# VectorE in source order in units 1 to 7 of a block-scheme MLP on one Trainium2 core

## The chip, the core and the metric

The kernel runs on one core of a Trainium2 chip. The metric is the device time of one execution in microseconds (us). TensorE (PE; its weight loads are listed apart, as PEld), VectorE (DVE), ScalarE (ACT), GpSimd (POOL) and SyncE (SP, here only the issuer of DMAs) run at the same time and wait for each other through semaphores. Each engine starts its own instructions in the order in which they stand in its queue.

## What is computed

Windowed attention, then an MLP over tokens and channels, then a normalised MLP over channels. The change touches only the last one:

```python
mu = np.mean(x, axis=-1, keepdims=True)
var = np.mean((x - mu) ** 2, axis=-1, keepdims=True)
xn = (x - mu) / np.sqrt(var + 1e-06) * g_ln
ch = np.maximum(xn @ w_ch1, 0.0) @ w_ch2      # 512 -> 2048 -> 512
return x + ch
```

with x of 2 x 768 rows and 512 channels, all in float32. On TensorE each float32 operand stands as a high and a low part, so one product takes three matmuls (`mm3`, L300 to L304).

## The kernel before

The normalised MLP is the second half of the program. Its 2048 hidden channels are cut into 8 pieces (`NP`), its rows into two halves; a **unit** is one piece for one half, so there are 16. Units 0 to 7 (`unit`, L770) take the first half, units 8 to 15 (`unit1`, L857) the second.

A unit of the first half forms its hidden block by a scheme of seven products of 2x2 blocks. Step k (0 to 6) issues product k (six matmuls of 384 columns into one PSUM bank, `product`, L755), then the readers of that bank, then `flow` (L818): two of the twelve `second` blocks (three matmuls of 512 columns each, for the second matrix of the unit before; one block only in steps 5 and 6), and then `step(k)` (L1265). The bank readers are: step 0 a copy on ACT (L787), all others adds of 384 columns on DVE (L775): `um` in step 1, `sm` in step 2, `wm` in step 3, `sm` in step 4, `wm` and `um` in step 5, `um` in step 6. After steps 2, 4, 5 and 6 a finished block goes through `relu` (L762): ACT writes the high part `ah` (L766), DVE the low part `al` (L767), which the next unit's `second` blocks read.

The products rotate over two PSUM banks (`ps_mm`), so product k+2 waits for the readers of product k. The transposes `tx` of `prep_x` (L595) take a bank of the same pool: in a step with a `tx` the next product comes back to the bank of the product just done.

`step(k)` holds the side work. `convert_all(2)` takes two pieces of the decoding and splitting of weights, which lasts until unit 2 (DVE: L150, L152, L156, L158, L237, L242, L247, the sums L265 to L271 and L282; ACT: L133 to L139, L209 to L213, L277; these last need spill buffers that a DMA to DRAM frees). `start` and `finish` take one piece of `bg`: in unit 1 the statistics `norm_stats` of groups 2 and 3 (L528; three BN_STATS with their aggregate, and then a chain of seven small operations of three columns, with a square root on ACT in it) and the first normalisation; in units 2 to 5, in steps 1 and 5, one piece of `prep_x` (L583): transposes on PE, then on ACT the copy `f` (L599), three normalisations of the next piece (L562) and one cast for each operand (L580), and on DVE the subtraction that gives its low part (L581) and the sums `t` (L610 to L622). From unit 2, step 6, `next(sums)` takes pieces of `w2_sums` (L715): seven pieces for each of the 8 parts, on DVE the sums `wx` (L726, from a weight tile that a DMA brought), `wt` (L735 to L738) and the low part `wk` (L748), whose DMA to DRAM stands behind it.

Who sets the order: PE and ACT stand under `manual_schedule` in this part (L1200, L1258), which puts them in the order of the source. DVE does not: there a scheduler orders the instructions at build time by priority and by its own estimate of when each is ready, and `high_priority(URGENT)` (L784) lifts the bank readers and `relu`. SP's order of DMAs is the scheduler's too.

Of the kernel before, what the change touches and what calls it, by code (L numbers as in the profile page):

```python
# [17 lines left out]
ALU = mybir.AluOpType  # L18
# [28 lines left out]
NP = F2 // 2  # L47
RING = 12
URGENT = 400
MS = ("B11", "T2", "B21", "T1", "B22", "T3", "T4")  # L50
EARLY = 16
NEG = -8e9
# [4 lines left out]
def f32(ap):  # L57
    return ap.bitcast(F32)


class Kern:
# [693 lines left out]
    def product(self, n, s, k, ps):  # L755
        w = self.ring_w1(n)
        x = self.operand(s, MS[k])
        for e in range(2):
# [3 lines left out]
    def relu(self, key, x):  # L762
        nc = self.nc
        ah = self.ap.tile([P, GN], F32R, tag="ah", name=f"ah_{key}")
        al = self.ap.tile([P, GN], F32R, tag="al", name=f"al_{key}")
        nc.scalar.activation(ah, x, AF.Relu)  # L766
        nc.vector.scalar_tensor_tensor(al, x, 0.0, f32(ah), op0=ALU.max, op1=ALU.subtract)  # L767
        return ah, al

    def unit(self, n, pending, step):  # L770
# [7 lines left out]
        for k in range(7):  # L778
# [4 lines left out]
            urgent = ExitStack()  # L783
            urgent.enter_context(self.tc.high_priority(URGENT))  # L784
            if k == 0:
# [57 lines left out]
    def pieces(self, name, x, relu=False):  # L843
        ah = self.ap.tile([P, GN], F32R, tag="ah", name=f"ah_{name}")
        al = self.ap.tile([P, GN], F32R, tag="al", name=f"al_{name}")
        self.cut(ah, al, x, relu)
        return ah, al

    def cut(self, hi, lo, x, relu):
        nc = self.nc  # L850
        nc.scalar.activation(hi, x, AF.Relu if relu else AF.Copy)
        if relu:
            nc.vector.scalar_tensor_tensor(lo, x, 0.0, f32(hi), op0=ALU.max, op1=ALU.subtract)
        else:
            nc.vector.tensor_tensor(lo, x, f32(hi), op=ALU.subtract)

    def unit1(self, n, pending, step):  # L857
# [8 lines left out]
        for k in range(7):  # L866
# [4 lines left out]
            urgent = ExitStack()  # L871
            urgent.enter_context(self.tc.high_priority(URGENT))
            if k == 0:
# [222 lines left out]
    def run(self):  # L1096
        tc, nc, ctx = self.tc, self.nc, self.ctx
# [73 lines left out]
        E = mybir.EngineType  # L1171
# [25 lines left out]
        later, pending = deque(), deque()  # L1197
# [63 lines left out]
        sums = (x for p in (2, 3, 4, 5, 0, 6, 1, 7) for x in self.w2_sums(p))  # L1261
        pending.popleft()()
        for n in range(2 * NP):

            def step(k):  # L1265
                if n == 0 and k == 6:
                    for r in range(9, RING):
                        self.load_w1(r)
                self.convert_all(2)
                if (n, k) == (4, 0):  # L1270
                    self.read_again(0)
                if n == 1 or n in range(2, 6) and k in (1, 5):
                    for _ in range(2 if n == 1 and k > 4 else 1):
                        self.start(1)
                        self.finish()

                if n > 2 or n == 2 and k > 5:
                    for _ in range((2, 0, 1, 2, 2, 0, 2)[k] if n < 6 else 2 if n == 7 or k in (0, 4) else 1):
                        next(sums, None)

            if n == 1:
                self.bg += [self.norm_stats(2)] * (GT + 1) + [self.norm_stats(3)] * (GT + 1)
                self.bg += [self.prep_x(1)] * 9
            pending = (self.unit1 if n >= NP else self.unit)(n, pending, step)
        self.tail(pending)


# [84 lines left out]
```

## Time and profile before

| | us |
|---|---|
| median of 3 runs (lowest, highest) | 580.86 (580.39, 584.26) |
| the profiled execution | 581.19 |
| its span, first to last instruction | 579.4 |
| PE busy in the span | 562.0 (97%) |
| DVE busy | 425.4 (73%) |
| ACT busy | 297.2 (51%) |

The page lists busy times by engine, then groups of instructions by line. The timeline gives single instructions with start, duration and, in brackets, the idle time of the engine before them and what ended it. Units 1 to 7 lie between 330.25 and 447.3 us of the span.

### The profile page before, as it was taken

The page shows a single profiled execution, that of the slowest core. Times are in us where ns is not written, and L with a number is a line of the kernel's source. Part 1 is how long each engine was busy: PE and PEld are TensorE (multiplying, and loading weights), DVE is VectorE, ACT ScalarE, POOL GpSimd, SP SyncE. Part 2 cuts the span into 40 slices and gives each one's busy share as a digit, 9 for nine tenths or more (in the row PEclk, how much of TensorE's full clock was granted, in tenths as well). Part 3 has the DMA queues.
Part 4 walks back from the last instruction along what each step waited for, and adds up shares of the span by engine and source line. Part 5 has one row for each costly group of instructions (what it writes and reads, how often), then busy time and mean ns, then how long its engine had stood idle before and what let it go on. Part 6 is the DMA issues. An engine that isn't in the chain of part 4 may idle for free.

```text
span 579.4 us, 10272 instructions
## 1 busy us (share of the span) xinstructions
PE 562.0 (97%) x3656; PEld 494.7 (85%) x3656; DVE 425.4 (73%) x1012; ACT 297.2 (51%) x629; POOL 22.2 (4%) x54
## 2 busy tenths in 40 slices
PE   8798998999999999999999999999999999999997
PEld 3465776889998889998988888888899999999997
DVE  5598966576887689756659898786986786677781
ACT  5598757326875654755578464463432232233320
POOL 0314400000000000000000000000000000000000
PEclk9799999999999999999999999999999999999999
DMA  8999910133668766788936899897988998777545
GB/s 278 330 315 286 282 66 2 33 113 110 229 206 271 255 219 232 274 314 290 326 111 234 278 325 334 268 334 233 306 261 280 329 292 297 237 226 232 186 155 172
DMA packets 61993, 137.88 MB, mean 238 GB/s; under 512 B 5875, under 2 KB 19955, under 8 KB 61942
## 3 DMA queue, kind: packets, MB, share of 16 engines
q1 hardware_dynamic: 61936, 137.21, 71.4%
q8 instruction: 29, 0.48, 0.3%
q14 instruction: 22, 0.18, 0.1%
q10 hardware_dynamic: 6, 0.02, 0.0%
HBM read 102.60 MB, written 34.60 MB: 237 GB/s over the span
## 4 chain that ended last, share of the span: by engine, by line
PE 80%; DVE 8%; DMA 6%; ACT 4%; issue 1%; POOL 0%; SPq 0%; DVEq 0%; ACTq 0%; POOLq 0%
PE m L302 6%; PE m L304 6%; PE m L303 6%; PE g L475 3%; PE acc_x L303 2%; PE acc_x L304 2%; PE acc_x L302 2%; DMA slot<-w2s 2%; PE acc_y L304 2%; PE acc_y L303 2%; PE acc_y L302 2%; PE av L446 2%; ACT pr L419 1%; DMA VT<-in_vt_dram 1%; PE scores L389 1%; PE g L302 1%
## 5 line engine op out<-in xcount | busy, mean ns | idle before, releaser
L302 PE MATMUL m<-slot,slot 128*128 128x384 f32 (+1 forms) x141 | 47.5, 337 | 1.4 <-DVE um L775 0.7
L304 PE MATMUL m<-slot,slot 128*128 128x384 f32 (+1 forms) x141 | 46.8, 332 | 0.0
L303 PE MATMUL m<-slot,slot 128*128 128x384 f32 (+1 forms) x141 | 46.8, 332 | 0.0
L303 PE MATMUL acc_x<-slot,ah 128*128 128x512 f32 x96 | 37.8, 394 | 0.0
L304 PE MATMUL acc_x<-slot,al 128*128 128x512 f32 x96 | 37.8, 394 | 0.0
L302 PE MATMUL acc_x<-slot,ah 128*128 128x512 f32 x96 | 37.6, 391 | 0.0
L419 ACT ACTIVATE pr<-sn,mn 128x120 f32<-128x120 f32 x96 | 30.2, 384 | 11.5 <-DVE mn L409 11.4
L302 PEld LDWEIGHTS m<-slot,slot 128*128 128x128 f32 x141 | 26.5, 188 | 4.4 <-DVE um L775 1.6
L303 PEld LDWEIGHTS m<-slot,slot 128*128 128x128 f32 x141 | 26.5, 188 | 1.6
L409 DVE CUSTOM_DVE_ANT_0 sn<-scores,mask 128x120 f32<-128x120 f32 x96 | 21.3, 276 | 7.8 <-PE scores L389 7.5
L304 PEld LDWEIGHTS m<-slot,slot 128*128 128x128 f32 x141 | 26.5, 188 | 0.0
L156 DVE SCALAR_TENSOR_TENSOR dec<-stage,dec 128x512 uint32<-128x512 uint32 x36 | 25.4, 705 | 0.4
L766 ACT ACTIVATE ah<-sm 128x384 fp32r<-128x384 f32 x16 | 8.4, 524 | 33.0 <-DVE sm L775 33.0
L152 DVE SCALAR_TENSOR_TENSOR dec<-stage,dec 128x512 uint32<-128x512 uint32 x36 | 24.8, 689 | 0.5
L133 ACT ACTIVATE dec<-stage 128x512 f32<-128x512 f32 x36 | 24.3, 674 | 0.0
L158 DVE SCALAR_TENSOR_TENSOR dec<-stage,dec 128x512 uint32<-128x512 uint32 x23 | 15.9, 690 | 9.5 <-ACT stage L139 9.4
L475 PE MATMUL g<-u,tok 128*128 128x256 f32 x96 | 22.5, 386 | 0.0
L304 PEld LDWEIGHTS acc_x<-slot,al 128*128 128x128 f32 x96 | 18.0, 188 | 4.0
L136 ACT ACTIVATE dec<-stage 128x512 f16<-128x512 f32 x23 | 18.4, 800 | 4.4 <-DMA stage<-in_wts_dram 4.3
L475 PEld LDWEIGHTS g<-u,tok 128*128 128x128 f32 x96 | 17.7, 190 | 2.9 <-issue 0.5
L304 PE MATMUL acc_y<-slot,al_s 128*128 128x256 f32 x72 | 20.1, 280 | 0.0
L303 PE MATMUL acc_y<-slot,ah_s 128*128 128x256 f32 x72 | 20.1, 279 | 0.0
(1492 smaller groups left out, 1759.2 us busy)
## 6 DMA issues: line engine op xcount, KB each, us to landing
stage<-in_wts_dram SPq DMA_DIRECT2D x62, 512.0 KB, 4.5
slot<-w1s SPq DMA_DIRECT2D x94, 256.0 KB, 4.0
w1s<-sps SPq DMA_DIRECT2D x16, 512.0 KB, 4.2
w2s<-sp SPq DMA_DIRECT2D x16, 512.0 KB, 2.8
slot<-w2s SPq DMA_DIRECT2D x16, 512.0 KB, 4.9
w2t<-wk SPq DMA_DIRECT2D x16, 512.0 KB, 4.9
slot<-w2t SPq DMA_DIRECT2D x8, 768.0 KB, 4.7
slot<-w2s SPq DMA_DIRECT2D x22, 256.0 KB, 4.3
```

The source lines that it names most:

```text
L133: nc.scalar.activation(m, high, AF.Abs, scale=2.0**-112)
L136: nc.scalar.activation(q[:, :, 1].bitcast(F16), high, AF.Copy, scale=2.0**-60)
L152: put(m, t[:, :, 1], 0x80000000, m, op0=ALU.bitwise_and, op1=ALU.bitwise_or)
L156: put(m, t[:, :, 0], 29, m, op0=ALU.logical_shift_right, op1=ALU.bitwise_or)
L158: put(m, t[:, :, 1], 3, m, op0=ALU.logical_shift_left, op1=ALU.bitwise_or)
L302: nc.tensor.matmul(out, lhs[0], rhs[0], start=first, stop=False)
L303: nc.tensor.matmul(out, lhs[0], rhs[1], start=False, stop=False)
L304: nc.tensor.matmul(out, lhs[1], rhs[0], start=False, stop=last)
L409: self.ttr[n] = nc.vector.tensor_tensor_reduce(sn[:, u], ps[:, u % 2, u // 2, :NK], self.mask[:, mv], scale=-SCALE, scalar=3e38, op0=ALU.a ...
L419: nc.scalar.activation(pr[:, u], sn[:, u], AF.Exp, bias=mn[:, u : u + 1], scale=-1.0)
L446: nc.tensor.matmul(ps[64 * j : 64 * j + 64, e, 65 * r : 65 * r + 65], pt[:, u * P + 64 * (r ^ j) : u * P + 64 * (r ^ j) + 64], V[:, j, 2 * ...
L475: nc.tensor.matmul(ps[:, :256], self.tok1(st, t), self.u[:, b * ST + st, 256 * hf : 256 * hf + 256], start=st == 0, stop=st == ST - 1,)
```

## The change

VectorE is put under `manual_schedule` too, for units 1 to 7 (`HAND <= n < NP`). In those units the low part of `relu` is not issued with `relu` but kept in a list, and `step` issues it after the two pieces of conversion and the pieces of `w2_sums`. The pieces of `w2_sums` move ahead of `start` and `finish`, and their counts change: in units 2 to 5 one piece in step 6 where there were two, in unit 6 two pieces in steps 0, 3 and 5 where it was 0 and 4. Unit 0 and units 8 to 15 stay under the scheduler.

```diff
+HAND = 1
...
         nc.scalar.activation(ah, x, AF.Relu)
-        nc.vector.scalar_tensor_tensor(al, x, 0.0, f32(ah), op0=ALU.max, op1=ALU.subtract)
+        low = lambda: nc.vector.scalar_tensor_tensor(al, x, 0.0, f32(ah), op0=ALU.max, op1=ALU.subtract)
+        if self.late is None:
+            low()
+        else:
+            self.late.append(low)
         return ah, al
...
                 if (n, k) == (4, 0):
                     self.read_again(0)
+                if n > 2 or n == 2 and k > 5:
+                    for _ in range((2, 0, 1, 2, 2, 0, 1)[k] if n < 6 else 2 if n == 7 or k in (0, 3, 5) else 1):
+                        next(sums, None)
+                for low in self.late or ():
+                    low()
+                if self.late:
+                    self.late.clear()
                 if n == 1 or n in range(2, 6) and k in (1, 5):
                     for _ in range(2 if n == 1 and k > 4 else 1):
                         self.start(1)
                         self.finish()
 
-                if n > 2 or n == 2 and k > 5:
-                    for _ in range((2, 0, 1, 2, 2, 0, 2)[k] if n < 6 else 2 if n == 7 or k in (0, 4) else 1):
-                        next(sums, None)
-
...
-            pending = (self.unit1 if n >= NP else self.unit)(n, pending, step)
+            with ExitStack() as hand:
+                self.late = None
+                if HAND <= n < NP:
+                    hand.enter_context(tc.manual_schedule(engines={E.DVE}))
+                    self.late = []
+                pending = (self.unit1 if n >= NP else self.unit)(n, pending, step)
```

## Rows read from the trace of the kernel before

**Rows 1.** The page, busy time of each engine in the span
```profile
PE 562.0 (97%) x3656; PEld 494.7 (85%) x3656; DVE 425.4 (73%) x1012; ACT 297.2 (51%) x629; POOL 22.2 (4%) x54
```
**Rows 2.** Windows of units 1, 2, 3, 4, 6: length, PE, PEld, DVE, ACT, POOL, clock, DMA
```profile
330.25:346.46 16.21, 15.89 (x77) 14.04 (x78) 15.03 (x36) 9.40 (x19) 0.00 (x0) 1.00 0.95 332
346.46:364.99 18.53, 16.86 (x87) 14.94 (x86) 16.08 (x40) 9.76 (x23) 0.00 (x0) 1.00 0.90 319
364.99:381.67 16.68, 16.59 (x86) 14.70 (x85) 11.37 (x23) 7.87 (x18) 0.00 (x0) 1.00 0.86 284
381.67:399.03 17.36, 16.61 (x86) 14.73 (x85) 13.02 (x26) 8.53 (x20) 0.00 (x0) 1.00 0.85 276
...
415.73:431.50 15.77, 15.77 (x80) 14.22 (x79) 13.44 (x28) 3.91 (x8) 0.00 (x0) 1.00 0.87 293
```
**Rows 3.** Timeline of PE's weight loads: those that waited (start, us, idle before)
```profile
335.74 0.19 PEld L302 LDWEIGHTS m<-slot,slot 128*128 128x128 f32 x1 [0.75 <-ACT sm L787]
...
363.14 0.19 PEld L302 LDWEIGHTS m<-slot,extra 128*128 128x128 f32 x1 [1.91 <-DVE um L775]
...
379.82 0.19 PEld L302 LDWEIGHTS m<-slot,slot 128*128 128x128 f32 x1 [0.33 <-DVE um L775]
...
397.18 0.19 PEld L302 LDWEIGHTS m<-slot,slot 128*128 128x128 f32 x1 [0.98 <-DVE um L775]
```
**Rows 4.** Timeline of PE: a second block, a product, the next block
```profile
380.97 0.39 PE L302 MATMUL acc_x<-slot,ah 128*128 128x512 f32 x1
...
381.67 0.33 PE L302 MATMUL m<-slot,slot 128*128 128x384 f32 x1
...
382.73 0.39 PE L302 MATMUL acc_x<-slot,ah 128*128 128x512 f32 x1
```
**Rows 5.** Timeline of DVE in unit 2
```profile
354.60 0.69 DVE L726 TENSOR_TENSOR wx<-slot 128x512 f32<-128x512 f32 x1 [1.79 <-DMA slot<-w2s]
355.21 0.55 DVE L775 TENSOR_TENSOR sm<-m,sm 128x384 f32<-128x384 f32 x1
...
362.07 0.55 DVE L775 TENSOR_TENSOR wm<-m,wm 128x384 f32<-128x384 f32 x1
362.54 0.55 DVE L775 TENSOR_TENSOR um<-m,um 128x384 f32<-128x384 f32 x1
```
**Rows 6.** Timeline of DVE, statistics of group 2: first BN_STATS, start and middle of chain
```profile
306.73 0.68 DVE L534 BATCH_NORM_STATS2 st<-u 128x6 f32<-128x512 f32 x1
...
314.07 0.17 DVE L544 TENSOR_SCALAR ve<-mv 128x3 f32<-128x3 f32 x1
...
341.46 0.18 DVE L546 RECIPROCAL r<-sd 128x3 f32<-128x3 f32 x1
```
**Rows 7.** Timeline of DVE: two independent adds, two of which the second reads the first
```profile
346.75 0.42 DVE L242 TENSOR_TENSOR sp<-dec,sp 128x256 fp32r<-128x256 f32 x1
347.08 0.42 DVE L265 TENSOR_TENSOR sa<-dec 128x256 f32<-128x256 f32 x1
...
358.42 0.41 DVE L737 TENSOR_TENSOR wt<-wt,wx 128x256 f32<-128x256 f32 x1
358.87 0.42 DVE L738 TENSOR_TENSOR wt<-wt,wx 128x256 f32<-128x256 f32 x1
```
**Rows 8.** Timeline of ACT: start of unit 1, and piece 2 of prep_x in unit 3
```profile
334.80 0.53 ACT L766 ACTIVATE ah<-um 128x384 fp32r<-128x384 f32 x1
335.21 0.48 ACT L787 COPY sm<-m 128x384 f32<-128x384 f32 x1
...
370.86 1.26 ACT L562 ACTIVATE xn<-u,nb,rs 128x128 f32<-128x128 f32 x3
372.01 0.50 ACT L580 CAST xt<-t_T 128x384 fp32r<-128x384 f32 x1
372.42 0.52 ACT L580 CAST xt<-f_B 128x384 fp32r<-128x384 f32 x1
```
**Rows 9.** Timeline of DVE: the last low part of unit 0
```profile
335.51 0.55 DVE L767 SCALAR_TENSOR_TENSOR al<-um,ah 128x384 fp32r<-128x384 f32 x1
```

## The prediction, made before the changed kernel ran

> **What bounds the kernel now.** I read the page first: PE is busy for 97% of the span [rows 1], so a change on DVE can pay or cost only through waits of PE. Then the windows by unit. Unit 6 has no transposes and no wait and takes 15.77 us; PE is busy in all of it [rows 2]. That is seven products of 1.06 and twelve second blocks of 0.70 [rows 4]. Units 2 to 5 add two transposes of some 0.36, so 16.5 is their floor; units 1, 2, 3 and 4 take 16.21, 18.53, 16.68 and 17.36 [rows 2], and 5 is like 3. Above the floor lie 0.4, 2.0, 0.2, 0.9 and 0.2 us: 3.7 in all, 0.6% of the time. A measurement of this kernel can tell about 1% (5.8 us) from no change, so no gain in these units can be that large. Third, the weight loads that waited [rows 3]: in unit 1, product 2 for ACT's copy (0.75); in units 2 to 5, product 6 for the second reader of step 5, `um` (1.91, 0.33, 0.98; unit 5 as unit 3). There the transpose has taken the other bank, so product 6 has to wait for both readers: 0.33 is left even when they start as soon as product 5 ends. Fourth, why unit 2 waits longer: the scheduler put `wx` ahead of `sm`, it stood 1.79 us for its DMA, and `wm` and `um` of step 5 came at 362.07 and 362.54 [rows 5], late by the 1.6 us that the weight load waited beyond 0.33.
>
> **The change part by part.** No instruction is added or removed; the order on DVE changes. Prices on DVE are start-to-start: 0.47 us for 384 columns (362.07 to 362.54) and 0.61 for 512 (354.60 to 355.21) [rows 5], 0.33 for 256 (346.75 to 347.08) [rows 7].
>
> *Gain, units 2 and 4.* In source order `wx` of part 2 comes in step 6 of unit 2, when its tile has long landed, and the readers of step 5 stand ahead of everything that is not needed first. Product 6 then waits 0.33: 1.6 less in unit 2, 0.65 less in unit 4. Sum -2.25.
>
> *Loss, unit 1.* The scheduler had pulled work out of unit 1. The BN_STATS of group 2 ran from 306.73, its variance at 314.07 [rows 6], both now in unit 1, where DVE already shows 15.03 us busy of 16.21 [rows 2]. I wrote the DVE instructions of unit 1 one below the other in source order. A BN_STATS takes 0.68 [rows 6], and its aggregate, which reads it, starts only at its end: 0.8 together, an estimate. An operation that reads the one just ahead starts 0.45 after it where an independent one starts after 0.33 [rows 7]: 0.12 more. The chain of seven small operations, of 0.17 or 0.18 each [rows 6], one waiting for the next and in the middle for ACT: no row has it in one piece. From below it costs 0.6 (seven starts of 0.09 between other work), from above 2.0 (seven whole durations, a wait of 0.05 each, and 0.4 for ACT); I take 1.5, near the top, since in source order nothing stands between its parts. Then, in us:
> step 1 (add, L158, L247, statistics) 2.5; step 2 (add, wait of 0.6 for `ah`, low, statistics) 2.4; step 3 (add, L150, L152, chain) 3.0; step 4 (add, L156, L237, low, statistics) 3.0; step 5 (two adds, L158, L242, low, two statistics) 3.9; step 6 (add, two sums, low, chain) 3.2; step 0 of unit 2, two sums, 0.7.
> PE needs 2.46 for each of steps 0 to 4 and 1.76 for 5 and 6 [rows 4]. Step 1 can't start before ACT's copy ends at 335.7 [rows 8]. So step 5 starts at 335.7 + 10.9 = 346.6, and its two adds end at 347.6; product 0 of unit 2, which reuses that bank, started at 346.46 [rows 2]: 1.1 late. Step 6 then starts at 350.5 and its add ends at 351.05; product 1 could start at 347.6 + 2.46 = 350.05: another 1.0. In step 6 ACT has the square root, three normalisations (1.16 [rows 8]) and only then the copy of product 0, at about 354.1; the transpose in step 1 of unit 2 waits for it, 0.6, and product 2 behind it for `um`, 0.4. Sum +3.1. From below the loss is 0.2 (with the cheap chain and cheap aggregates the queue is 2.5 us shorter and only ACT's copy is late), from above 5.2 (the second rival).
>
> *Loss, units 3 to 6.* In steps 1 and 5 the DVE parts of `prep_x` now stand ahead of the next bank reader, and they wait for ACT, which does three normalisations (1.16) and a cast of 0.41 for each operand first [rows 8]. After piece 2 (unit 3, step 1) `sm` of step 2 starts some 3 us after its product ends; 3.85 are allowed before product 4 waits, so nothing stops, but steps 2 to 4 with four sums win back only 2.4 of it, and the readers of step 5 are 0.5 late. After piece 3 (step 5) `um` of step 6 comes 2.8 us late and holds product 1 of unit 4 for 0.4 and product 2 for 0.3. Unit 5 has the same pieces with one `wx` more in step 3: 1.2 and then 0.35. Sum 0.5 + 0.7 + 1.2 + 0.35 = +2.75. From below 0 (the lag is always won back), from above 4.
>
> *The low parts of relu.* Four of 0.47 in each unit, moved behind the side work of their own step. The second blocks that read them come a unit later; the cover is that unit, and nothing waits. SP's DMAs of `wk` and of the conversion move back by up to 4 us with their DVE instructions, and loads of the ring queue behind them; a ring tile is loaded twelve products, some 27 us, ahead. I take 0 for both; if that cover went, each late load would show as a PE wait on a DMA. The last pieces of `w2_sums` slide three places into unit 8, where DVE has room: 0.
>
> Sum: -2.25 + 3.1 + 2.75 = +3.6 us. The profiled execution took 581.19 (span 579.4 and 1.8 around it), so 584.8; it lies 0.33 over the median of the runs, so against that **584.4**, 0.6% more.
>
> **A rule weighed.** The row shows that a reader of the result just ahead starts 0.12 later than an independent operation [rows 7]. The Trainium skill, "VectorE: DVE Perf Modes", section "The DRAIN you can't avoid", holds that the pipe is flushed after every operation and that a semaphore after each costs nothing extra. By it the 17 such steps in units 1 and 2 would be free, some 2.0 us off DVE's queue, and the sum would be +1.6. I keep the row.
>
> **Rivals.**
> *A gain.* DVE stays inside the slack of the banks in unit 1. For it: units 1 and 2 together, 34.7 us, hold 31.1 busy [rows 2], and overlapping durations count twice, so the room is there, only later. Against it: the room is in unit 2, and the queue is no longer free to put it off. It decides in step 5 of unit 1: if `um` there ends before 346.4 instead of 347.6, unit 1 passes its lag on to unit 2. Then the gains of 2.25 stand nearly alone: about 578.9.
> *Unit 0's rest first.* If the hand-ordered queue starts only behind the last instruction of unit 0, the low part at 335.51 [rows 9], which waits for `ah` (334.80 [rows 8]), then L156, L247 and one BN_STATS of step 0 (2.0) come after it and not in the idle time before the copy. All of unit 1 on DVE lies 2.1 later, and PE with it: 586.5. For it: a queue by source order; against it: only instructions inside the block need be tied.
> *No effect.* The readers are urgent already, and the new order differs in little that PE sees: what unit 1 loses, unit 2 gives back, and units 3 to 6 win back their lag. 580.9. For it: units 6 and 7 run without a wait under the present order. Against it: the group 2 statistics have to go somewhere.
>
> **How the numbers follow.** Forecast 0.42 (its own range 582 to 586.5), gain 0.20, unit 0's rest first 0.20, no effect 0.13, anything else 0.05. The range: the gain case with 0.4 below it, 578.5; above, the second rival and 1.5 for the upper bounds, 588. Slower by over 1% is over 586.7: half of the second rival (0.10), an eighth of the forecast (0.05), the rest (0.03): 0.18. Faster by over 1% can't come out of 3.7 us; 0.02 for what I don't see. Within 1%: 0.80.
>
> **What would show it.** Right: product 6 of units 2 and 4 waits about 0.3; new waits on `um` at products 0, 1 and 2 of unit 2; 0.4 to 1.5 at product 6 of units 3 and 5 and at product 1 of units 4 and 6; no DVE wait on a DMA ahead of a reader; units 6 and 7 near 15.8. Wrong: unit 2's first products wait for nothing, or PE waits for DMAs or for a low part, or the time moves in units 8 to 15, where nothing was reordered.

## The result, and the profile after

The changed kernel takes 588.14 us (median of 6 runs, 586.53 to 589.68), the kernel before, run beside it, 581.57 (6 runs). The ratio is 1.0106, 95% interval 1.0083 to 1.0129: slower by 4.8 to 7.5 us. The forecast was 584.4 with a range up to 588: the sign was right, the size too small, and the time lies just above the range. The profiled execution took 587.77 (span 586.0) against 581.19 (579.4): +6.6 us of span.

Where the 6.6 us went is read from PE's timeline, by the start of product 0 of each unit. Unit 1 begins at 331.75 instead of 330.25: 1.50 us are lost ahead of the changed units (the last section says where). Units 8 to 15 and the tail take 132.2 us in both. The rest:

| kernel | units 1 and 2 | 3 to 6 | 7 | 1 to 7 | ratio of the runs, 95% |
|---|---|---|---|---|---|
| before | 16.45 + 18.28 | 66.48 | 15.68 | 116.9 | 1 |
| after | 18.19 + 18.99 | 69.14 | 15.69 | 122.0 | 1.0106 (1.0083 to 1.0129) |

(By the first matmul of product 0, unit 2 of the kernel before begins at 346.70. The windows of [rows 2] are cut at its weight load, 346.46, which is why they have 16.21 and 18.53 for units 1 and 2.)

So the change costs 5.1 us in units 1 to 6. The page has PE at 96%; DVE's work is the same as before, 426.2 for 425.4 [rows 1]:

```profile
PE 564.6 (96%) x3651; PEld 495.1 (84%) x3656; DVE 426.2 (73%) x1012; ACT 297.3 (51%) x629; POOL 22.2 (4%) x54
```

(Lines of the program stand a little lower than before: L780 are the bank readers, L768 the low part, L792 the copy, L582 the low part of `prep_x`, L535 and L536 the statistics.) The windows of units 1 to 6 answer to [rows 2], with the same columns:

```profile
331.75:349.94 18.19, 16.46 (x78) 13.88 (x78) 15.79 (x38) 8.45 (x18) 0.00 (x0) 1.00 0.98 326
349.94:368.93 18.99, 17.46 (x84) 14.71 (x85) 16.57 (x40) 10.47 (x25) 0.00 (x0) 1.00 0.86 292
368.93:386.37 17.44, 16.82 (x85) 14.64 (x84) 10.86 (x22) 7.99 (x18) 0.00 (x0) 1.00 0.91 303
386.37:403.90 17.53, 17.14 (x85) 14.69 (x84) 13.92 (x28) 8.72 (x20) 0.00 (x0) 1.00 0.74 231
403.90:421.94 18.04, 16.80 (x85) 14.62 (x84) 12.50 (x25) 7.87 (x17) 0.00 (x0) 1.00 0.67 219
421.94:438.07 16.13, 16.02 (x80) 14.11 (x78) 13.11 (x26) 5.05 (x10) 0.00 (x0) 1.00 0.82 274
```

The weight loads of PE that waited [rows 3] are the list by which the forecast wanted to be judged (start, us, idle before and its releaser):

```profile
346.55 0.19 PEld L303 LDWEIGHTS m<-slot,slot 128*128 128x128 f32 x1 [0.52 <-DVE sm L780]
...
349.94 0.19 PEld L303 LDWEIGHTS m<-slot,slot 128*128 128x128 f32 x1 [1.82 <-DVE um L780]
...
353.40 0.19 PEld L303 LDWEIGHTS m<-slot,slot 128*128 128x128 f32 x1 [1.19 <-DVE um L780]
...
356.70 0.31 PEld L596 LDWEIGHTS tx<-ident,xn 128*128 128x128 f32 x3 [1.03 <-ACT sm L792]
...
357.31 0.19 PEld L303 LDWEIGHTS m<-slot,slot 128*128 128x128 f32 x1 [0.30 <-DVE um L780]
...
367.08 0.19 PEld L303 LDWEIGHTS m<-slot,extra 128*128 128x128 f32 x1 [0.33 <-DVE um L780]
...
379.12 0.19 PEld L303 LDWEIGHTS m<-slot,slot 128*128 128x128 f32 x1 [0.38 <-DVE sm L780]
...
384.51 0.19 PEld L303 LDWEIGHTS m<-slot,slot 128*128 128x128 f32 x1 [0.86 <-DVE um L780]
...
389.10 0.19 PEld L303 LDWEIGHTS m<-slot,slot 128*128 128x128 f32 x1 [0.55 <-DVE um L780]
...
392.30 0.19 PEld L303 LDWEIGHTS m<-slot,slot 128*128 128x128 f32 x1 [0.40 <-DVE um L780]
...
402.04 0.19 PEld L303 LDWEIGHTS m<-slot,slot 128*128 128x128 f32 x1 [0.33 <-DVE um L780]
...
414.09 0.19 PEld L303 LDWEIGHTS m<-slot,slot 128*128 128x128 f32 x1 [0.38 <-DVE sm L780]
...
420.10 0.19 PEld L303 LDWEIGHTS m<-slot,slot 128*128 128x128 f32 x1 [1.48 <-DVE um L780]
...
424.66 0.19 PEld L303 LDWEIGHTS m<-slot,extra 128*128 128x128 f32 x1 [0.54 <-DVE um L780]
```

Three blocks of lines. From 346.55 to 357.31, unit 1's lag: the end of unit 1 and products 0, 1 and 2 of unit 2 with its transpose. At 367.08 and 402.04 the gain: product 6 of units 2 and 4 waits 0.33 instead of 1.91 and 0.98. From 379.12 on, the lag behind `prep_x`.

How unit 1 falls behind is seen in DVE's timeline, at its start and in its step 3:

```profile
334.93 0.69 DVE L248 TENSOR_TENSOR sp<-dec,sp 128x512 fp32r<-128x512 f32 x1
336.74 0.56 DVE L768 SCALAR_TENSOR_TENSOR al<-um,ah 128x384 fp32r<-128x384 f32 x1 [1.13 <-ACT ah L767]
337.22 0.69 DVE L535 BATCH_NORM_STATS2 st<-u 128x6 f32<-128x512 f32 x1
337.94 0.18 DVE L536 BATCH_NORM_AGGREGATE mv<-st 128x2 f32<-128x6 f32 x1
338.04 0.54 DVE L780 TENSOR_TENSOR um<-m,sm 128x384 f32<-128x384 f32 x1
...
344.42 0.16 DVE L545 TENSOR_SCALAR ve<-mv 128x3 f32<-128x3 f32 x1
344.86 0.18 DVE L547 RECIPROCAL r<-sd 128x3 f32<-128x3 f32 x1 [0.27 <-ACT sd L546]
...
345.87 0.16 DVE L553 SCALAR_TENSOR_TENSOR nb<-mv,rs 128x3 f32<-128x3 f32 x1
345.94 0.55 DVE L780 TENSOR_TENSOR sm<-m,wm 128x384 f32<-128x384 f32 x1
```

DVE stands idle for 1.13 ahead of unit 0's last low part [rows 9], then runs a BN_STATS with its aggregate (0.82 from start to start of the next), and only then `um` of step 1, 6.29 after the start of the unit. (In the kernel before, `um` of step 1 started 6.33 after it and cost nothing, as less stood behind it.) ACT's copy, which `um` reads, had ended 5.32 after the start:

```profile
336.20 0.51 ACT L767 ACTIVATE ah<-um 128x384 fp32r<-128x384 f32 x1
336.62 0.45 ACT L792 COPY sm<-m 128x384 f32<-128x384 f32 x1
```

The chain of small operations [rows 6] stands in one piece now, 344.42 to 345.94, with `sm` of step 4 behind it.

Where unit 1 meets unit 2 the trace does not have the order of the source. Group 3's chain, from step 6 of unit 1, is interleaved with a sum of step 0 of unit 2, and with the first `wx` of part 2, which stands in step 6 of unit 2 in the source and yet ran ahead of `um` of step 1:

```profile
355.26 0.66 DVE L727 TENSOR_TENSOR wx<-slot 128x512 f32<-128x512 f32 x1
...
356.70 0.56 DVE L780 TENSOR_TENSOR um<-m,sm 128x384 f32<-128x384 f32 x1
```

Here it waited for nothing. Why it stands there no run shows.

In unit 3, DVE's queue stands for 3.27 us at a low part of `prep_x`, with `sm` of step 2 behind it, and by step 5 `um` is still late:

```profile
376.50 0.56 DVE L582 TENSOR_TENSOR xt<-t_T,xt 128x384 fp32r<-128x384 f32 x1 [3.27 <-ACT xt L581]
...
378.51 0.55 DVE L780 TENSOR_TENSOR sm<-m,sm 128x384 f32<-128x384 f32 x1
...
383.91 0.54 DVE L780 TENSOR_TENSOR um<-m,um 128x384 f32<-128x384 f32 x1
```

### The profile page after: what moved, and what is told of

Its sections match the earlier page's. It is cut to its first block, busy times and chain, and to the rows that moved or that the text cites. A ratio compares the mean times of both kernels' runs of the same rounds, so it can differ in the third digit from the quotient of the medians.

```text
span 586.0 us, 10273 instructions
## 1 busy us (share of the span) xinstructions
PE 564.6 (96%) x3651; PEld 495.1 (84%) x3656; DVE 426.2 (73%) x1012; ACT 297.3 (51%) x629; POOL 22.2 (4%) x54
## 4 chain that ended last, share of the span: by engine, by line
PE 77%; DVE 11%; ACT 6%; DMA 3%; issue 1%; POOL 0%; SPq 0%; ACTq 0%; DVEq 0%; POOLq 0%
PE m L303 6%; PE m L305 5%; PE m L304 5%; PE g L476 3%; PE acc_x L304 2%; PE acc_x L305 2%; PE acc_x L303 2%; PE acc_y L305 2%; PE acc_y L304 2%; PE acc_y L303 2%; ACT pr L420 2%; PE av L447 1%; DMA VT<-in_vt_dram 1%; PE scores L390 1%; PE g L303 1%
```

## The experiments

Two theories were to be told apart, each with a rival. **A:** the loss in units 1 and 2 is the work that stands in front of the readers in unit 1, the statistics above all; rivals: the source order of the rest, the low part of unit 0. **B:** the loss in units 3 to 6 is the DVE parts of `prep_x` in front of the readers; rival: the new places of the `w2_sums` pieces. Each time is given as length of units 1 to 7 in the profile (before 116.9, after 122.0), and the ratio to the kernel before on the same chip.

**Unit 1 back under the scheduler.**

```diff
-HAND = 1
+HAND = 2
```

> VectorE tied to source order in units 2 to 7 only. Units 1 to 7 (product 0 of unit 1 to product 0 of unit 8) take 116.9 us before and 122.0 after the change. Theory A (the statistics, which the scheduler had run from 306 on, now stand in unit 1 and make its bank readers late): with unit 1 free again, unit 1 takes 16.4 as before, unit 2 loses only its old wait at product 6 (-1.6), units 3 to 6 stay as after (+2.7): units 1 to 7 take 118.0, ratio about 1.002. Rival (the order inside unit 2 is what makes products 0 to 2 of unit 2 wait): these waits stay, 3 us or more, units 1 to 7 take 120 or more, ratio 1.006.

118.9; 584.46 us, ratio 1.0038 (1.0015 to 1.0062). The waits at products 0 to 2 of unit 2 are gone, units 1 and 2 take 16.49 + 17.54. But product 6 of unit 2 waits 0.94, not 0.33. DVE shows why:

```profile
354.60 0.69 DVE L727 TENSOR_TENSOR wx<-slot 128x512 f32<-128x512 f32 x1 [2.99 <-DMA slot<-w2s]
355.21 0.55 DVE L582 TENSOR_TENSOR xt<-f_B,xt 128x384 fp32r<-128x384 f32 x1
355.68 0.55 DVE L780 TENSOR_TENSOR sm<-m,sm 128x384 f32<-128x384 f32 x1
```

With PE on time, this `wx` waits 2.99 for its weight tile, as it waited 1.79 in the kernel before [rows 5], and the low part of `prep_x` and `sm` of step 2 stand behind it. ACT's cast for that low part had ended at 353.64, so the hold is the `wx`. The forecast's gain of 1.6 in unit 2 thus hangs on when this tile lands.

**Statistics out of unit 1's end, and prep_x held back.** In the first kernel group 2's statistics stand ahead of unit 0 and group 3's in steps 0 to 3 of unit 1; in the second the DVE parts of `prep_x` (with the last of them one cast on ACT too) are kept in a list, and the next step issues them, behind its readers; the third has both.

```diff
-                if n == 1 or n in range(2, 6) and k in (1, 5):
-                    for _ in range(2 if n == 1 and k > 4 else 1):
...
+                if n == 1 and k in (0, 1, 2, 3, 6) or n in range(2, 6) and k in (1, 5):
...
+            if n == 0:
+                for _ in self.norm_stats(2):
+                    pass
```

> As the changed kernel, but the statistics of group 2 are issued before unit 0, outside the tied part, and those of group 3 one piece a step in steps 0 to 3 of unit 1, so that some 4 us of VectorE work leave unit 1. Theory A: the waits at products 0, 1 and 2 of unit 2 (3.8 us together after the change) fall under 0.5, units 1 and 2 lose the old 1.6 at product 6, units 1 to 7 take 118.0 to 118.6, ratio 1.002. Rival (unit 1 is late because unit 0's last low part and ACT's copy come late): products 0 to 2 of unit 2 still wait 2 us or more, units 1 to 7 take 120.5 or more.

121.2; ratio 1.0058 (1.0036 to 1.008). Unit 2 fell to 16.72, as theory A has it, but unit 1 rose to 19.68, 3.2 more than before. ACT's timeline shows where the first half of that comes from:

```profile
332.68 0.62 ACT L214 CAST sp<-dec 128x512 fp32r<-128x512 f32 x1 [3.91 <-DMA w1s<-sps]
...
335.42 0.46 ACT L792 COPY sm<-m 128x384 f32<-128x384 f32 x1
```

The statistics moved DVE's work in unit 0, the spill DMA was issued 1.4 later against the start of unit 1 (0.67 ahead of it instead of 2.08), and ACT stood 3.91 us for it with the copy of product 0 behind; product 2 waited 2.47 and started 1.7 later in the unit than before. The second half is the clock: behind that wait it fell, the granted clock of unit 1 is 0.91, and product 3 started another 1.5 later. A PE that is late by itself also gives DVE time, so the missing waits at the start of unit 2 do not show theory A. The edit brought a wait of its own and sizes nothing.

```diff
-        nc.vector.tensor_tensor(lo[e], x, f32(hi[e]), op=ALU.subtract)
+        self.put(lambda: nc.vector.tensor_tensor(lo[e], x, f32(hi[e]), op=ALU.subtract))
...
             def step(k):
+                self.release()
```

> As the changed kernel, but the VectorE parts of prep_x are held back one step, behind that step's bank readers; ACT's order stays. Theory B (these parts, waiting for three normalisations and the casts on ACT, stand ahead of the next readers): product 6 of units 3 and 5 waits 0.33, products 1 and 2 of unit 4 and product 1 of unit 6 wait for nothing, units 3 to 6 lose 3.3 against after; units 1 to 7 take 118.7, ratio about 1.003. Rival (the pieces of w2_sums fill the steps before product 6): product 6 of units 3 and 5 still waits 0.8 and 1.5, the time stays at ratio 1.009.

120.3; ratio 1.0064 (1.004 to 1.0088). Units 3 to 6 fell from 69.14 to 67.12. The waits at product 4 of units 3 and 5 and at product 1 of units 4 and 6 are gone; product 2 of unit 4 still waits 0.19, and product 6 of units 3 and 5 0.60 and 1.13. Theory B holds for 2.0 of its 3.3 us.

> The two edits together: statistics out of unit 1, VectorE parts of prep_x held back one step. Theories A and B: only the gains are left, -1.6 at product 6 of unit 2 and -0.65 at product 6 of unit 4, so units 1 to 7 take 114.5 to 115.5 against 116.9 before, ratio 0.996 to 0.998. Rival (tied order costs VectorE time of its own, where an operation waits for the one just ahead): 117 or more, ratio 1.000 or above.

119.1; ratio 1.0044 (1.0021 to 1.0066): unit 1 19.42 with ACT's wait as above (3.77 for the DMA, 2.32 at product 2), units 3 to 6 67.15. A miss, by the wait that the moved statistics bring: here, with the clock at 1.00, DVE's readers came late behind it, 0.88 at product 6 of unit 1 and 1.01 at product 0 of unit 2.

**Statistics left out.** First group 2's, then group 3's too.

```diff
+                self.stats[2] = self.stats[1]
...
-                self.bg += [self.norm_stats(2)] * (GT + 1) + [self.norm_stats(3)] * (GT + 1)
+                self.bg += [iter(range(8))] * (GT + 1) + [self.norm_stats(3)] * (GT + 1)
```

> The changed kernel without the statistics of group 2 (three BN_STATS with their aggregates and the chain of small operations; group 2 is normalised with the numbers of group 1 instead, so that part of the computation is left out). PE's order and every other DVE instruction stand as in the changed kernel, where units 1 to 7 took 122.0 us, units 1 and 2 37.2 of it. Theory A (the loss of unit 1 is the 3.9 us of statistics that stand in front of the readers): units 1 and 2 fall to 33.2 to 33.8, no weight load of products 0 to 2 of unit 2 waits, units 3 to 7 stay; units 1 to 7 118.0 to 118.6, time about 584.5. Rival B (it is the source order of the other instructions in unit 1 and the low part of unit 0 in front of them): units 1 and 2 stay above 35.5, the waits at the start of unit 2 are still there with some 1 us, time about 587.

119.6; ratio 1.006 (1.0035 to 1.0086). Units 1 and 2 took 34.83, between the theories: 2.35 came back, not 3.4 or more. What I had left out is that group 3's statistics stand in steps 4 to 6. Three waits are left at the start of unit 2, on product 1 (0.59), the transpose (1.04) and product 2 (0.28); the expectation of the next run calls the first of them product 0.

> The changed kernel without the statistics of groups 2 and 3 (both groups are normalised with the numbers of group 1, so that part of the computation is left out; the normalisations themselves stay). Without group 2's alone units 1 and 2 took 34.8 us instead of 37.2, and three waits were left at the start of unit 2 (0.59 at product 0, 1.04 at the transpose, 0.28 at product 2). Theory (these three come from group 3's statistics in steps 4 to 6: two BN_STATS with aggregates ahead of um in step 6, and the chain with its square root ahead of ACT's normalisation and copy): all three vanish, units 1 and 2 take 33.1 to 33.4, units 1 to 7 118.0 to 118.3. Rival (the three normalisations on ACT, which stay, or the sums and conversions of steps 5 and 6, hold the copy by themselves): the transpose still waits 0.7 or more and units 1 and 2 stay at 34 or above.

118.0; ratio 1.0029 (0.9998 to 1.0059). Units 1 and 2 took 16.51 + 16.71 = 33.2. Of PE's weight loads in units 1 and 2, behind product 0 of unit 1, only these two waited:

```profile
338.22 0.19 PEld L303 LDWEIGHTS m<-slot,slot 128*128 128x128 f32 x1 [0.90 <-ACT sm L792]
...
364.02 0.19 PEld L303 LDWEIGHTS m<-slot,extra 128*128 128x128 f32 x1 [0.33 <-DVE um L780]
```

The first is the old wait for ACT's copy in unit 1, the second product 6 of unit 2. Theory A is shown in this sense: without the statistics the source order of the rest of unit 1 costs nothing, 37.18 - 33.22 = 3.96 us come back, and with unit 1 under the scheduler the same statistics cost nothing either (16.49 in the run above). By the prices of the changed kernel (0.82 and 1.52) the two groups are some 8 us of DVE's queue, so leaving out as much of other work might have freed it too; no run tells that apart.

**The hole at the start of unit 1.** One instruction moved: unit 0's last low part goes behind the first BN_STATS.

```diff
+                if (n, k) == (1, 0):
+                    for low in self.late:
+                        low()
+                    self.late.clear()
```

> The changed kernel with one instruction moved: the last low part of unit 0 is issued behind the first BN_STATS of unit 1 instead of ahead of it, so that the 1.13 us in which DVE waited for ACT's high part are filled with 0.8 us of statistics. Theory (unit 1's DVE queue has no slack left, so a hole at its start is paid for at its end): units 1 and 2 fall by 0.8, from 37.2 to 36.4, and product 0 of unit 2 waits for um 1.0 instead of 1.8. Rival (the hole is hidden, the queue catches up before it reaches a bank that PE needs): 37.2 again.

122.0; ratio 1.0126 (1.0093 to 1.0158). In that profile ACT waited 2.72 instead of 2.07 for the spill DMA and its copy ended 0.67 later, so the kernel was run once more:

> A second look at the kernel with the last low part of unit 0 behind the first BN_STATS of unit 1. In its first profile a DMA that ACT waits for ended 0.66 us later than in the profile of the changed kernel, so that ACT's copy of product 0 ended 6.0 after the start of unit 1 instead of 5.3, and what the move gave could not be seen. Theory: where the copy ends at 5.3, um starts at 5.5 instead of 6.3 and units 1 and 2 take 36.4. Rival: 37.2 again at a copy of 5.3. If the copy is late again, moving the instruction itself makes that DMA late, and the hole at the start of unit 1 is not a loss that can be taken out alone.

121.4, one run, 584.93. The copy ended 5.30 after the start of unit 1, and DVE shows

```profile
333.27 0.69 DVE L535 BATCH_NORM_STATS2 st<-u 128x6 f32<-128x512 f32 x1
333.99 0.18 DVE L536 BATCH_NORM_AGGREGATE mv<-st 128x2 f32<-128x6 f32 x1
334.46 0.56 DVE L768 SCALAR_TENSOR_TENSOR al<-um,ah 128x384 fp32r<-128x384 f32 x1 [0.29 <-ACT ah L767]
335.15 0.56 DVE L780 TENSOR_TENSOR um<-m,sm 128x384 f32<-128x384 f32 x1
```

`um` starts 5.66 after the start instead of 6.29, and units 1 and 2 take 36.67 instead of 37.18. So 0.5 of the loss is the hole, in this one trace. What went is the wait of 0.52 at product 6 of unit 1; product 0 of unit 2 still waits 1.71, not the 1.0 of the theory. Whole runs do not resolve it.

**Relu's low parts at once.**

```diff
-                    self.late = []
+                    self.late = None
```

> The changed kernel with relu's low part issued at once behind relu, as before the change, VectorE still in the order of the source. Theory (in source order an early low part waits for ACT's high part at the head of DVE's queue, and in step 5 um stands behind it: wm to um 1.5 us instead of 0.47): product 6 of units 2 to 5 waits 1.1 us more in each (1.4 in units 2 and 4), units 1 and 2 lose another 1.1 to 1.7 in steps 4 and 5; units 1 to 7 126 to 129 instead of 122.0, time about 593. Rival (the low parts have cover wherever they stand, as I took in the forecast for the move itself): 122.0 within 0.5.

132.2; 597.94 us, ratio 1.0262 (1.0192 to 1.0331). The rival is out; the time is more than the theory's 126 to 129. DVE in step 5 of unit 2:

```profile
367.73 0.55 DVE L780 TENSOR_TENSOR wm<-m,wm 128x384 f32<-128x384 f32 x1
368.87 0.56 DVE L768 SCALAR_TENSOR_TENSOR al<-wm,ah 128x384 fp32r<-128x384 f32 x1 [0.59 <-ACT ah L767]
369.34 0.55 DVE L780 TENSOR_TENSOR um<-m,um 128x384 f32<-128x384 f32 x1
```

1.61 from `wm` to `um` instead of 0.47. But the 10.2 us over the changed kernel are not waits alone. Product 0 of unit 2 waits 3.63 for 1.82, and behind that wait PE runs slower:

```profile
351.09 0.69 PE L303 MATMUL m<-slot,slot 128*128 128x384 f32 x1 [3.19 <-DVE um L780]
...
353.18 0.63 PE L303 MATMUL acc_x<-slot,ah 128*128 128x512 f32 x1
```

This product takes 2.09 and the two second blocks behind it 2.56, where [rows 4] have 1.06 and 1.40; the granted clock of unit 2 is 0.86. It fell again behind the wait of product 6 of unit 5. By the starts in PE's timeline the slower work costs 4.1 us in the two places. The other 6.1 are waits, so that without the clock it would be 128.1, inside the theory's range. Their path is not quite the theory's: product 6 of units 2 to 5 (1.12, 2.79, 1.27, 3.32) waits for ACT's copy of the transpose, not for `um`:

```profile
369.35 0.19 PEld L303 LDWEIGHTS m<-slot,extra 128*128 128x128 f32 x1 [1.12 <-ACT f_B L600]
```

Moving the low parts back is thus worth 6 us of waits in source order, and in this profile 4 more by the clock.

**Only the new places of the w2_sums pieces**, with VectorE under the scheduler everywhere.

```diff
-HAND = 1
+HAND = NP
```

> The changed source with VectorE under the scheduler in all units (low parts at once), so that of the change only the new place and counts of the pieces of w2_sums are left. Theory (what costs and what gains is the order on VectorE, not the place of these pieces in the source): units 1 to 7 take 116.9 within 0.4, product 6 of unit 2 waits about 1.9 and of unit 4 about 1.0 as before, units 6 and 7 15.7, time equal to the kernel before. Rival (the new counts alone delay the sums or their DMAs): units 3 to 7 longer by 1 us or more, or PE waits for a weight tile in units 6 to 8.

117.6; ratio 1.0012 (0.9986 to 1.0038). 0.3 outside of what I wrote: product 6 of unit 2 waits 2.35. Units 3 to 6 take 66.39, before 66.48: the pieces alone cost nothing there, so the loss of units 3 to 6 is the order on VectorE.

**Both undoings**: `HAND = 2` and the held `prep_x`; then also the pieces spread evenly.

> Both partial undoings together: unit 1 back under the scheduler, and the DVE parts of prep_x one step behind the readers. If the two losses are separate and add, units 1 to 7 take what the two runs gave alone: 118.9 for unit 1 under the scheduler, less the 1.8 to 2.0 that prep_x gave back in units 3 to 6, 116.9 to 117.1, which is the kernel before (116.9): time equal to it within 0.5 us. If they share a cause (one frees the room that the other uses), units 1 to 7 come out above 118.

115.9; 581.5 us, ratio 1.001 (0.9989 to 1.0031). A microsecond better in the trace than the sum of the two, since holding `prep_x` back also frees unit 2 (16.71 for 17.54: `sm` of step 2 now runs ahead of the `wx`, and product 6 waits 0.33 and not 0.94). The runs do not show that microsecond.

```diff
-                    for _ in range((2, 0, 1, 2, 2, 0, 1)[k] if n < 6 else 2 if n == 7 or k in (0, 3, 5) else 1):
+                    for _ in range((2, 1, 1, 1, 1, 1, 1)[k] if n < 6 else 2 if n == 7 or k in (0, 3, 5) else 1):
```

> As the run with both undoings, and the pieces of w2_sums spread evenly over units 3 to 5: one piece in each of steps 1 to 6 and two in step 0, where steps 3 and 4 had two and steps 1 and 5 none. Theory (what is left at product 6 of units 3 and 5, 0.60 and 1.13 instead of 0.33, is the lag of steps 2 to 4 that the doubled pieces keep up): product 6 waits 0.33 to 0.45 in both, units 1 to 7 take 115.8 to 116.2, about 1 us less than the kernel before. Rival (wx now comes before its weight tile, or another wait takes the place): a wait of DVE for a DMA in units 3 to 5, and 117 or more.

115.0, 0.8 under what I wrote; 580.93 us against 581.8, ratio 0.9986 (0.9968 to 1.0003). Product 6 now waits for both readers and no longer, in units 3 and 5 as in 2 and 4:

```profile
363.55 0.19 PEld L303 LDWEIGHTS m<-slot,extra 128*128 128x128 f32 x1 [0.33 <-DVE um L799]
...
380.24 0.19 PEld L303 LDWEIGHTS m<-slot,slot 128*128 128x128 f32 x1 [0.33 <-DVE um L799]
...
397.19 0.19 PEld L303 LDWEIGHTS m<-slot,slot 128*128 128x128 f32 x1 [0.33 <-DVE um L799]
...
413.89 0.19 PEld L303 LDWEIGHTS m<-slot,slot 128*128 128x128 f32 x1 [0.33 <-DVE um L799]
```

This version is the one that uses the change's idea without its two losses: 1.9 us shorter than before in units 1 to 7 of the trace. By the runs it lies between 1.9 us faster and 0.2 slower, so that it beats the kernel before is likely and not shown.

## Why the prediction was too small

The mechanism of the losses was right; two terms of the sum were too small, the gain in unit 2 came out by luck, and a further share came from outside of the change.

| term | forecast | measured |
|---|---|---|
| gain, unit 2 and unit 4 | -1.6, -0.65 | 1.91 to 0.33, 0.98 to 0.33: -2.23 |
| loss of unit 1: product 0, product 1, transpose and product 2 | 1.1, 1.0, 1.0 | 1.86, 1.02, 1.22 less 0.1 ahead: 4.0 |
| loss, units 3, 4, 5, 6 | 0.5, 0.7, 1.2, 0.35 | 0.75, 0.83, 1.33, 0.40: 3.3 |
| sum | +3.6 | +5.1 |

The measured column is made from the starts of the products in PE's timeline.

- *Unit 1: the step that failed* is "Step 1 can't start before ACT's copy ends at 335.7", taken as the time when it does start (5.45 into the unit). It started at 6.29. The statistics of step 0 were to fill the time before the copy, as the price list of the steps has none for step 0; but they stood behind unit 0's last low part, which waits for ACT, and came behind the copy. The 0.84 arrive at product 0. It began 1.74 late; the forecast's own times give 0.9 against the matmul at 346.70 (its 1.1 is counted from the weight load at 346.46), and the table's 1.86 takes in that product 2 was 0.1 early. My second rival named this place, but as all or nothing: 2.1 us with two conversions and the BN_STATS. The trace shows the conversions ahead of the low part and only the statistics behind it. When the order was changed there, 0.5 us came back, in one profile. The other two rivals are out: units 1 to 6 all came out longer than before.
- The other prices in unit 1 hold: BN_STATS with aggregate 0.82 (0.8), the chain 1.52 (1.5), and product 1's extra 1.02 (1.0). Leaving the statistics out gave the whole loss back: 3.96. The first rival's room was read too large: in the windows overlapping durations count once, not twice (the durations of DVE in unit 1 [rows 2] add up to 17.4, the row has 15.03).
- *Gain in unit 2: right in size, by luck.* "In source order `wx` of part 2 comes in step 6 of unit 2" was wrong. It ran ahead of `um` of step 1, as shown above, and waited for nothing there, where everything was 3 to 4 us late and the tile had landed. With unit 1 on time it waited for the tile again: 2.99 and 0.94 at product 6 with unit 1 under the scheduler, 1.97 and the bare 0.33 without the statistics.
- *Units 3 to 6: mis-sized*, 3.3 for 2.75. "So nothing stops" was wrong: `sm` of step 2 started 3.4 after its product ended, not 3, and product 4 of units 3 and 5 waited 0.38. Each unit's term came out a little over the forecast's.
- *The low parts of relu* were costed at 0 for the move, with the unit as cover. In the sum that is right, but the reason was incomplete: in source order an early low part costs 6 us of waits, and in the profile 4 more by the clock, while units 6 and 7 of the kernel before have early low parts under the scheduler and no wait.
- *The rule weighed*: the Trainium skill, "VectorE: DVE Perf Modes", section "The DRAIN you can't avoid", would have made the sum +1.6. The trace stays with the row: in the chain each operation of 0.16 starts 0.19 to 0.21 after the one that it reads, while `um` starts 0.10 after an aggregate of 0.18 that it does not read.
- Of the difference between 584.4 and 588.14, 1.5 us are these terms, 0.7 is the kernel before itself (580.86 in the runs shown, 581.57 beside the changed kernel). The remaining 1.5 is as large as what the profiled execution lost ahead of unit 1. That the six runs lost it there too is an inference, since the profile is of one of them. The mean granted clock fits it: five of the six show the 0.991 of the profiled one, the profile before has 0.994, and the sixth, with 0.997, is the fastest.

## What to carry to other kernels

Source order on an in-order engine is right only if nothing near the head of the queue waits for another engine: before writing it by hand, list for each side instruction whom it waits for and which reader stands behind it, and put it behind that reader. When a queue is full from end to end, a hole of a microsecond at its start is paid for at its end, at least in part (here 0.63 us at the start gave back 0.5). Work that a scheduler had pulled forward (here group 2's statistics, some 4 us) must be given a place by hand, or the new order pays for it (2.35 us for that group, 3.96 with group 3's). And the order that was written is to be read again in the trace: one `wx` stood elsewhere.

## What the runs showed of the hardware

Ahead of unit 1, PE's and DVE's instructions are the same before and after, and yet the profiled executions differ by 1.5 us there. PE waits 1.68 us for DVE at a transpose, in the kernel before at 93.84 and in the changed one at 93.80; from there to unit 1 it takes 236.41 and 237.95. The windows from 90 to 100 us of the kernel before, and then of the changed kernel, differ in the granted clock:

```profile
90.00:100.00 10.00, 8.28 (x131) 6.43 (x129) 7.08 (x34) 8.93 (x25) 0.00 (x0) 1.00 0.01 2
```

```profile
90.00:100.00 10.00, 8.32 (x111) 6.55 (x110) 6.69 (x33) 7.55 (x21) 0.00 (x0) 0.83 0.01 2
```

1.00 is the level of 2.4 GHz throughout; 0.83 is a stretch partly at 1.2. It happens or not after the same wait, whatever the kernel: in the profiles in which the work up to unit 1 is unchanged, the way from that transpose to unit 1 is 236.1 to 236.5 us at 1.00 (six of them, the kernel before included) and 237.7 to 238.4 at 0.83 (six, the changed kernel included). Half of what looked like the change's excess over the forecast in the profile was this.

Waits inside units 1 to 7 did the same. The clock fell at product 0 of unit 2 (a wait of 3.63) and behind product 6 of unit 5 (3.32) with the low parts at once, and behind product 2 of unit 1 (2.47) with the statistics moved; behind product 6 of unit 3 (2.79) and, with both edits, product 2 of unit 1 (2.32) it did not. A wait that an edit makes can thus cost PE's speed after it as well, and a profile's time must be read with the clock of the same window.

A DMA's landing moved by 0.7 us between two executions of one kernel, the one with the moved low part, on two chips (ACT's wait for the spill 2.72 and 2.02), which hid in the first of them what the move gave.
